# Moving left sums of a Strassen-like output product behind its first additions, in a windowed attention and gated feed-forward kernel

## The chip, the cores and the metric

The kernel runs on one core of one Trainium2 chip. The time is the device time of one execution in microseconds (us). The kernel before takes 333.5 us, the median of three runs (333.36 to 333.51). The engines are PE (matrix products), DVE (vector), ACT (activation functions and copies), Pool (a slower vector engine that also issues some DMAs) and SP (issues DMAs). Each engine works through its own queue in program order and waits on semaphores for the others.

## The reference

```python
# q, k, v: (8 batches, 8 heads, 576 positions, 64)
scores = q @ k^T / 8
scores = where(0 <= rel < 128, scores - slope[h] * |rel|, -1e9)   # rel = row - column
attn = softmax(scores);  x = (attn @ v) as (4608 tokens, 512)
out = (gelu(x @ w_gate) * (x @ w_val)) @ w_out                    # 512 -> 1536 -> 512
```

## The kernel before, in words

The 4608 tokens are worked off in nine groups `g` = 0 to 8 of 512 tokens. A group has a hidden stage (`x` times the gate and value weights, gelu, product; the result is `hT`, called `hid[g]`, twelve blocks `f` of 128 hidden features) and an output stage (`hid` times `w_out`). The attention of batch `b = g + 2` is spread over the output stage of group `g`, so that PE has work while others finish. One group takes about 34.6 us in the middle of the kernel.

**Hidden stage.** Blocks `f` are made one by one by `gate_val` (lines 642 to 673: eight matmuls, a gelu on ACT, a multiplication on DVE, line 667), except four blocks 6 to 9, which `gate_quad` (lines 822 to 892) makes together in seven products instead of eight. For these seven it needs sums of `x`: `combine_x` (lines 794 to 800, four additions t1 to t4, of which t2 needs t1 and t4 needs t2, on Pool in groups 2 to 6, written into the part of `left` for block pairs 3 to 5) and sums of weights, `combine_weights` (lines 772 to 781; those for blocks 0 to 3, which groups 7 and 8 use, are eight additions on Pool at the end of group 6's hidden stage). The last two multiplications of the four blocks run on Pool (lines 887 and 889).

**Output stage.** In groups 2 to 8 `out_products` (lines 1161 to 1270) also makes seven products (1 to 7) in place of eight, for each of two halves `a` = 0, 1 of the token pairs; six matmuls each (`product`, lines 752 to 763). With a11, a12, a21, a22 the quarters of `hid` (first index: lower or upper 256 tokens; second: even or odd block), `combine_left` (lines 729 to 737) makes four sums, each over six block pairs `i`, of which a call makes `lo` to `hi`:

```python
    steps = ((s1, a21, a22, ALU.add), (s2, s1, a11, ALU.subtract),
             (s4, a12, s2, ALU.subtract), (a21, a11, a21, ALU.subtract))
```

I call them sum 0, 1, 2 and 3, in the order of this line. Products 1 and 2 need no sum; product 6 needs sum 1, product 5 needs sum 0, product 7 needs sum 3, and product 3 needs sum 2. In groups 2 to 6 Pool makes all four sums of block pairs 0 and 1 behind `f` = 3 and sums 0 and 1 of pair 2 behind `f` = 5; DVE makes the rest after `f` = 11: sums 0 and 1 of pairs 3 to 5 (width 768), then sums 3 and 2 of pairs 2 to 5 (width 1024).

**Order of the output stage, groups 2 to 5** (line 1176 on, PE's order): products 1 and 2 of half 0, the first scores of the next batch (`scores2`, line 307), products 6, 5, 7 of half 0, product 1 of half 1, products 4 and 3 of half 0, the second scores, products 2, 6, 5, 7 of half 1, attention times values (`values`, line 508), products 4, 3 of half 1. Behind the products `gather_out` (lines 902 to 925) carries out of the PSUM banks: `p1` (909), `c11` (913, on DVE, an addition; it also frees the bank of product 2), `u2` (911), `p5` (917, on ACT), `c22` (919, on DVE; it reads the bank into which product 4 is then accumulated), `c21` (921) and `c12` (924). There are eight PSUM banks, handed on in turn, so a product or a score waits for an earlier reader of its bank. ACT's exponentials of the scores (line 236) and DVE's decay masks (line 241) lie in between. Group 6 has no scores of its own and another order (lines 1180 to 1213).

**Queues.** Pool's queue holds, in groups 2 to 5: a small copy `mark` (line 1328) that waits for block `f` = 3 of `hid`, the sums of `x`, its left sums, the two multiplications of the four blocks, and then the issue of fifteen loads of q, k and v (line 117; in group 5 only the five of v). In group 6, instead of loads: another `mark` (line 1352) that waits for sum 2, and the eight sums of weights. The normalizing factors of the attention (`rb`) are spread over the partitions by two DMAs from ACT's queue (line 463) and used by DVE (line 567).

Of the kernel before, what the change touches and what calls it, by code (L numbers as in the profile page):

```python
# [36 lines left out]
def kernel(  # L37
# [10 lines left out]
    nc = tc.nc  # L48
    B, H, S, D = q.shape
# [49 lines left out]
    mark = consts.tile([1, 2], BF16, name="mark")  # L99
# [353 lines left out]
    def gather(b):  # L453
        flat[b] = d_pool.tile([H, S], FP32, name="rd")
        for s in (0, 1):
            lo, w = shape(b, s)
            nc.scalar.dma_start(
                out=flat[b][:, lo:lo + 2 * w].rearrange("h (x t) -> x h t", x=2),
                in_=sumrow[b][0:128:8, lo:lo + w])
# [701 lines left out]
    def out_products(g):  # L1161
        b = g + 2
        O = lambda what, a, copy=act: gather_out(g, a, what, copy)
        P = lambda n, a: product(g, n, a)
        if b > B:
            for n, after in ((1, ("p1",)), (2, ()), (6, ("u2", "c11")), (5, ("p5",)), (7, ("c22",)), (4, ("c21",)),
                             (3, ("c12",))):
                for a in (0, 1):
                    P(n, a)
                    for what in after:  # L1170
                        O(what, a)
                store()
                if n == 6 and g + 1 < NG:
                    combine_x(g + 1)
            return
        P(1, 0)
        P(2, 0)
        O("p1", 0)
        urgent = 512 * (g + 2) - S * (b - 1)
        if b == B:  # L1180
            P(6, 0)
            O("u2", 0)
            O("c11", 0)
            P(5, 0)
            O("p5", 0)
            P(7, 0)
            O("c22", 0)
            scale = values(b - 1, later=True)
            P(4, 0)
            O("c21", 0)  # L1190
            P(3, 0)
            scale[0]()
            scale[1]()
            O("c12", 0)
            P(1, 1)
            O("p1", 1)
            store()
            P(2, 1)
            for do in scale[2:]:
                do()  # L1200
            O("c11", 1)
            P(6, 1)
            O("u2", 1)
            P(5, 1)
            O("p5", 1)
            P(7, 1)
            O("c22", 1)
            P(3, 1)
            O("c12", 1)
            P(4, 1)  # L1210
            O("c21", 1)
            combine_x(g + 1, 192, 256)
            return
        exp_table()
        O("c11", 0)
        later = []
        scores2(b, 0, later)
        A = later[0]
        P(6, 0)
        O("u2", 0, dve)  # L1220
        P(5, 0)
        for n in (0, 1, 3):
            A[n]()
        O("p5", 0)
        A[2]()
        P(7, 0)
        O("c22", 0)
        A[4]()
        for n in (5, 6, 7):
            A[n]()  # L1230
        P(1, 1)
        P(4, 0)
        P(3, 0)
        O("p1", 1)
        O("c21", 0)
        O("c12", 0)
        A[8]()
        A[9]()
        scores2(b, 2, later)
        A = later[1]  # L1240
        P(2, 1)
        P(6, 1)
        O("u2", 1, dve)
        O("c11", 1)
        add(b, 0, None, (0,))
        P(5, 1)
        for n in (0, 1, 3, 5):
            A[n]()
        O("p5", 1)
        A[2]()  # L1250
        P(7, 1)
        O("c22", 1)
        A[4]()
        for n in (6, 7):
            A[n]()
        store()
        scale, more = values(b - 1, urgent=urgent)
        for do in scale:
            do()
        P(4, 1)  # L1260
        P(3, 1)
        O("c21", 1)
        for do in more:
            do()
        O("c12", 1)
        A[8]()
        A[9]()
        add(b, 0, None, (2,))
        put_off.update({0: lambda: add(b, 0, act, (1,)), 1: lambda: add(b, 2, None, (0, 2)),
                        2: lambda: add(b, 2, act, (1,))})  # L1270
# [3 lines left out]
    for g in range(NG):  # L1274
        if 1 <= g < B - 2:
            transposes_dma(3 if g == 1 else g + 2)
        if g >= B - 1:
            for f in range(NF):
                if f in QUADS:
                    gate_quad(g, f)  # L1280
                elif not any(f0 < f < f0 + 4 for f0 in QUADS):
                    gate_val(g, f)
                if f == 4:
                    store()
                if f == 5:
                    combine_left(g, 0, 2, (0, 1), engine=nc.gpsimd)
                if f == 6:
                    combine_left(g, 2, 3, (0, 1))
                    combine_left(g, 0, 2, (3, 2), engine=nc.gpsimd)
            for which in ((0, 1), (3,), (2,)):  # L1290
                for lo, hi in ((3, 5), (5, 6)) if 0 in which else ((2, 5), (5, 6)):
                    combine_left(g, lo, hi, which)
            out_products(g)
            continue
        if g == 1:
            room = rooms(1)
            sums = combine_weights(6, nc.vector)
            for do in sums[:5]:
                do()
        for f in range(9 if g == 0 else 0, NF):  # L1300
            if f == 6 and g:
                gate_quad(g, 6, room if g == 1 else None,
                          (lambda: gather(g + 1)) if g in (2, B - 2) else None)
            elif not (g and 6 < f < 10):
                gate_val(g, f)
            if g == 1:
                for do in {0: sums[5:7], 1: sums[7:]}.get(f, ()):
                    do()
                if f in (1, 2, 3):
                    combine_x(1, 0, 256, {1: (0,), 2: (1, 2), 3: (3,)}[f])  # L1310
                if f in (4, 5, 10, 11):
                    combine_right({4: 0, 5: 1, 10: 2, 11: 3}[f])
            if f in put_off:
                put_off.pop(f)()
            if f == 1:
                store()
            if g == 0 and f == 10:
                masks_of_last_blocks(0, 8)
            if g == 0 and f == 9:
                for c in range(4):  # L1320
                    for w in (0, 1):
                        transpose(1, w, c, (act, dve)[w])
            if g < 2:
                continue
            if g == 2 and f == 2:
                add(3, 2, act, (1,))
            if f == 3:
                nc.gpsimd.tensor_copy(out=mark, in_=hid[g][0:1, f, 510:512])  # L1328
                combine_x(g, engine=nc.gpsimd)
                combine_left(g, 0, 2, (0, 1, 3, 2), engine=nc.gpsimd)  # L1330
            if f == (5 if g == 2 else 4):
                sums4(g + 1)
            if f == 5:
                combine_left(g, 2, 3, (0, 1), engine=nc.gpsimd)
                if 2 < g < B - 2:
                    gather(g + 1)
            if g == B - 2 and f == 2:
                combine_x(g + 1, 0, 192)
            if f == (11 if g == 2 else 6):
                spread_dma(g + 1)  # L1340
            if f == 6:
                if g + 3 < B:
                    load_qk(g + 3)
                if g + 2 < B:
                    load_v(g + 2)
            if f == 11:
                combine_left(g, 3, 6, (0, 1))
                for n in (3, 2):
                    combine_left(g, 2, 6, (n,))
        if g == B - 2:  # L1350
            sums = combine_weights(0)
            nc.gpsimd.tensor_copy(out=mark, in_=left[0:1, 2, 5, 0:2])
            for do in sums:
                do()
        if g == 1:
            nc.gpsimd.tensor_copy(out=mark, in_=kT[1][0:1, 0, 512:514])
            load_qk(4)
            load_v(3)
        if g == 0:
            nc.gpsimd.memset(Ps[0][:, :, 0:64], 0.0)  # L1360
            for t in (qs[1], ks[1]):
                nc.gpsimd.memset(t[64:128, 4, :], 0.0)
        if g in PRODUCTS:
            out_products(g)
        else:
            for item in steps(g):
                if isinstance(item, int):
                    out_part(g, item)
                else:
                    RUN[item[0]](*item[1:])  # L1370
            store()
        if g == 0:
            load_v(2)
            nc.gpsimd.tensor_copy(out=mark, in_=qT[0][0:1, 0, 512:514])
            load_qk(3)
# [30 lines left out]
```

## Time and profile before

| What | Value |
|---|---|
| time, median of 3 runs | 333.5 us (333.36 to 333.51) |
| the profiled execution: its own time | 333.97 us |
| its span, first to last instruction | 332.2 us |
| mean granted clock of PE | 0.995 |
| PE busy | 319.4 us (96%) |
| DVE busy | 255.4 us (77%) |
| ACT busy | 219.6 us (66%) |
| Pool busy | 200.3 us (60%) |

A line of a timeline gives the start in us from the span's start, the duration, the engine, the line of the kernel, the operation, what it writes and reads with the shape, the number of merged instructions (xN), and in brackets how long the engine stood idle before and what released it. Merged neighbours can overlap. A line of the windows gives a stretch, its length, then for each engine the busy time and instruction count, the granted clock, the DMA share and the rate.

Where the groups' output stages lie in this execution: product 6 of half 0 begins at 119.53 (group 2), 157.52 (group 3), 192.19 (group 4), 226.86 (group 5) and 260.63 us (group 6).

### The profile page before, as it was taken

The numbers are of one execution on the slowest core, as the hardware profiler recorded it, in microseconds if no ns is written. First come the engines' busy times: TensorE is split into PE (matmuls) and PEld (weight loads), VectorE is DVE, ScalarE is ACT, GpSimd is POOL, SyncE is SP. The second block draws the span as 40 slices with busy tenths as digits, with TensorE's granted clock in tenths as the row PEclk, the third lists the DMA queues.
The fourth block names the chain that finished last, engine by engine and source line by source line (L and its number), as shares of the span: only waits on it lengthen the run. The fifth ranks groups of instructions, "written<-read, shape, count | busy, mean of one in ns | idle before, by whom it ended". The sixth has DMA issues, their size and how long they took to land.

```text
span 332.2 us, 9496 instructions
## 1 busy us (share of the span) xinstructions
PE 319.4 (96%) x3784; PEld 216.7 (65%) x3784; DVE 255.4 (77%) x506; ACT 219.6 (66%) x417; POOL 200.3 (60%) x232
## 2 busy tenths in 40 slices
PE   8999999999999979999999999999999899999996
PEld 6566645574544748566765776577747687788765
DVE  7788766788789856977698669967898676785692
ACT  7974687568797656757875687577767237736641
POOL 6974689192096999079935994496019684420550
PEclk9999999999999989999999999999999999999999
DMA  8999999999799989954997499639200530003003
GB/s 215 168 197 190 203 168 183 130 211 136 137 170 127 181 159 191 168 131 100 174 197 115 129 178 192 131 106 190 99 34 5 142 129 3 0 2 127 3 0 126
DMA packets 149920, 43.57 MB, mean 131 GB/s; under 512 B 133588, under 2 KB 142964, under 8 KB 149876
## 3 DMA queue, kind: packets, MB, share of 16 engines
q0 software_dynamic: 107456, 18.10, 73.7%
q1 hardware_dynamic: 39104, 18.55, 25.9%
q10 hardware_dynamic: 3316, 6.32, 8.2%
q8 instruction: 29, 0.48, 0.6%
q14 instruction: 15, 0.12, 0.1%
HBM read 43.65 MB, written 9.53 MB: 160 GB/s over the span
## 4 chain that ended last, share of the span: by engine, by line
PE 49%; DVE 6%; POOL 4%; ACT 2%; issue 1%; DVEq 0%; POOLq 0%
PE ps L659 17%; PE ps L762 16%; PE ps L842 13%; DVE left L737 2%; PE ps L508 2%; DVE hT L667 1%; POOL left L800 1%; POOL left L737 1%; ACT P L236 1%; PE ps L307 1%; DVE xT L567 1%; POOL hT L887 1%; PE ps L444 1%; DVE P L241 1%; ACT osb L917 0%
## 5 line engine op out<-in xcount | busy, mean ns | idle before, releaser
L659 PE MATMUL ps<-xT,wg 128*128 128x512 bf16 (+4 forms) x312 | 71.8, 352 | 0.0
L659 PE MATMUL ps<-xT,wv 128*128 128x512 bf16 (+4 forms) x312 | 71.7, 352 | 0.0
L666 ACT ACTIVATE gelu<-ps 128x512 bf16<-128x512 f32 (+3 forms) x77 | 41.6, 546 | 35.1 <-PE ps L659 32.1
L667 DVE TENSOR_TENSOR hT<-ps,gelu 128x512 bf16<-128x512 f32 (+3 forms) x77 | 46.6, 623 | 18.3 <-PE ps L659 10.9
L236 ACT ACTIVATE P<-ps 128x512 bf16<-128x512 f32 (+1 forms) x108 | 52.2, 572 | 5.2 <-PE ps L307 3.1
L659 PEld LDWEIGHTS <-wv 128*128 128x128 bf16 x312 | 29.4, 98 | 29.8 <-DVE xT L567 0.2
L659 PEld LDWEIGHTS <-wg 128*128 128x128 bf16 x312 | 28.8, 98 | 25.9
L117 POOL DMA_DIRECT2D vb<-in_v_dram x40 | 34.1, 896 | 5.7 <-DMA ks<-in_k_dram 1.7
L241 DVE TENSOR_TENSOR P<-P,emask 128x768 bf16<-128x768 bf16 x60 | 32.0, 554 | 7.2 <-ACT P L236 5.4
L762 PEld LDWEIGHTS <-hT 128*128 128x128 bf16 x336 | 32.6, 99 | 7.1 <-issue 0.4
L762 PEld LDWEIGHTS <-left 128*128 128x128 bf16 x252 | 24.2, 98 | 10.3 <-issue 4.1
L1328 POOL COPY mark<-hT 1x2 bf16<-1x2 bf16 x5 | 0.9, 174 | 47.6 <-DVE hT L667 47.6
L887 POOL TENSOR_TENSOR hT<-qT,qs 128x512 bf16<-128x512 f32 x10 | 11.5, 1167 | 30.1 <-ACT qs L853 30.1
L762 PE MATMUL ps<-right,left 128*128 128x256 bf16 x168 | 22.0, 278 | 5.6 <-DVE osb L913 3.4
L842 PEld LDWEIGHTS <-kept 128*128 128x128 bf16 x256 | 25.1, 98 | 3.4 <-issue 0.6
L117 POOL DMA_DIRECT2D qs<-in_q_dram x30 | 25.4, 865 | 1.8 <-DMA wo<-in_moe_w_out_dram 1.0
L117 POOL DMA_DIRECT2D ks<-in_k_dram x30 | 25.4, 897 | 0.0
L762 PE MATMUL ps<-right,hT 128*128 128x256 bf16 x168 | 22.9, 278 | 0.2 <-DVE osb L919 0.2
L762 PE MATMUL ps<-wo,hT 128*128 128x256 bf16 x168 | 21.3, 275 | 0.0
L850 DVE TENSOR_TENSOR P<-ps,P 128x512 f32<-128x512 f32 x24 | 15.0, 682 | 6.8 <-PE ps L842 4.9
L850 DVE TENSOR_TENSOR qT<-ps,qT 128x512 f32<-128x512 f32 x20 | 12.9, 686 | 9.1 <-PE ps L842 7.7
L508 PE MATMUL ps<-P,vb 64*64 64x192 bf16 (+2 forms) x752 | 18.4, 221 | 1.5 <-ACT P L236 0.7
(170 smaller groups left out, 627.8 us busy)
## 6 DMA issues: line engine op xcount, KB each, us to landing
out_dram<-osb SPq DMA_DIRECT2D x34, 256.0 KB
rb<-rd ACTq DMA_DIRECT2D x10, 576.0 KB
vb<-in_v_dram POOLq DMA_DIRECT2D x32, 128.0 KB, 6.9
qs<-in_q_dram POOLq DMA_DIRECT2D x24, 128.0 KB, 5.5
ks<-in_k_dram POOLq DMA_DIRECT2D x24, 128.0 KB, 6.8
wo<-in_moe_w_out_dram POOLq DMA_DIRECT2D x4, 384.0 KB, 13.2
wg<-in_moe_w_gate_dram POOLq DMA_DIRECT2D x5, 256.0 KB, 8.4
wv<-in_moe_w_val_dram POOLq DMA_DIRECT2D x5, 256.0 KB, 9.0
```

Source lines behind the costliest of these rows:

```text
L117: nc.gpsimd.dma_start(out=t[at:at + n, j, :].rearrange("p (h d) -> p h d", h=H), in_=src[b][:, 128 * j:128 * j + n, :].rearrange("h p d -> ...
L236: nc.scalar.activation(out=dst, in_=src, func=AF.Exp, scale=0.125)
L241: nc.vector.tensor_tensor(out=dst, in0=dst, in1=m, op=ALU.mult)
L508: mm = nc.tensor.matmul(out=out, lhsT=lhsT, rhs=prob(b)[half, c, i, col:col + q1 - q0], start=all(t[2] != u for t in todo[:n]), stop=True, ...
L659: nc.tensor.matmul(out=ps[:, a:e], lhsT=w[:, c, 128 * f:128 * (f + 1)], rhs=xT[:, c, t0 + lo + a:t0 + lo + e], start=begins and a == 0, st ...
L666: nc.scalar.activation(out=gl[:, 0:n], in_=pg, func=AF.Gelu)
L667: nc.vector.tensor_tensor(out=hid[g][:, f, lo:hi], in0=pv, in1=gl[:, 0:n], op=ALU.mult)
L737: engine.tensor_tensor(out=to, in0=a, in1=b, op=op)
L762: nc.tensor.matmul(out=made[g, a, into], lhsT=lhsT, rhs=rhs, start=first and i == 0, stop=i == NF // 2 - 1, skip_group_check=True)
L842: nc.tensor.matmul(out=ps[:, 256 * e:256 * e + 256], lhsT=w[:, c, at:at + 128], rhs=x[:, c, :], start=n in (1, 2, 5) and e == 0 and c == 0 ...
L850: nc.vector.tensor_tensor(out=to[u], in0=cut(banks[n, u], to[u].shape[1]), in1=to[u], op=ALU.add)
L887: nc.gpsimd.tensor_tensor(out=out, in0=P5[u], in1=high, op=ALU.mult)
```

## The change

In groups 2 and 6 Pool no longer makes sums 3 and 2 of block pairs 0 and 1; it makes sums 0 and 1 of pairs 0 to 2 in one call behind `f` = 5. DVE makes sums 3 and 2 there for all six pairs (width 1536 instead of 1024). In groups 2 to 6 DVE's sums 3 and 2 no longer follow sums 0 and 1 directly: sum 3 stands behind `c11` of half 0, and sum 2 behind `u2` of half 0 (in group 6 both behind `c11`). In group 2 the sums of `x` are let go on Pool behind `f` = 0 instead of `f` = 3. In group 6 the `mark` and the sums of weights move with sum 2 into the output stage.

```diff
@@ out_products, b == B (group 6)
             P(6, 0)
             O("u2", 0)
             O("c11", 0)
+            for n in (3, 2):
+                combine_left(g, 0, 6, (n,))
+            nc.gpsimd.tensor_copy(out=mark, in_=left[0:1, 2, 5, 0:2])
+            for do in combine_weights(0):
+                do()
             P(5, 0)
@@ out_products, groups 2 to 5
         exp_table()
         O("c11", 0)
+        lo = 0 if g == 2 else 2
+        combine_left(g, lo, 6, (3,))
         later = []
         scores2(b, 0, later)
         A = later[0]
         P(6, 0)
         O("u2", 0, dve)
+        combine_left(g, lo, 6, (2,))
         P(5, 0)
@@ the hidden stage of groups 2 to 6
-            if f == 3:
+            if f == (0 if g == 2 else 3):
                 nc.gpsimd.tensor_copy(out=mark, in_=hid[g][0:1, f, 510:512])
                 combine_x(g, engine=nc.gpsimd)
+            if f == 3 and 2 < g < B - 2:
                 combine_left(g, 0, 2, (0, 1, 3, 2), engine=nc.gpsimd)
             if f == (5 if g == 2 else 4):
                 sums4(g + 1)
             if f == 5:
-                combine_left(g, 2, 3, (0, 1), engine=nc.gpsimd)
                 if 2 < g < B - 2:
+                    combine_left(g, 2, 3, (0, 1), engine=nc.gpsimd)
                     gather(g + 1)
+                else:
+                    combine_left(g, 0, 3, (0, 1), engine=nc.gpsimd)
@@
             if f == 11:
                 combine_left(g, 3, 6, (0, 1))
-                for n in (3, 2):
-                    combine_left(g, 2, 6, (n,))
-        if g == B - 2:
-            sums = combine_weights(0)
-            nc.gpsimd.tensor_copy(out=mark, in_=left[0:1, 2, 5, 0:2])
-            for do in sums:
-                do()
```

## The prediction

> **What bounds the kernel now.** I read first which waits PE has, because PE is busy nearly throughout and every stall of it counts at once.
>
> ```profile
> PE ps L762 <- DVE osb L913: 3.4, 4, 1.0
> PE ps L762 <- DVE left L737: 2.3, 2, 1.2
> ```
>
> The columns are the waiting engine, tile and line, what it waited for, the total in us, the times, and the longest. Both entries lie in output stages (line 762) and end on DVE: four times a product waits until `c11` (line 913) has freed its bank, twice it waits for left sums (line 737). That is 5.7 us, and the four and the two fit groups 2 to 5 and groups 2 and 6. So I read these stages in the timeline, first group 2.
>
> ```profile
> 106.19 0.69 POOL L117 DMA_DIRECT2D vb<-in_v_dram  x1 [1.40 <-DMA ks<-in_k_dram]
> ...
> 111.64 1.16 POOL L737 TENSOR_TENSOR left<-hT 128x512 bf16<-128x512 bf16 x1
> ...
> 113.33 2.19 ACT L853 ACTIVATE vb<-P 128x512 bf16<-128x512 f32 x4 [1.14 <-DVE P L850]
> ...
> 116.97 0.67 POOL L737 TENSOR_TENSOR left<-left,hT 128x256 bf16<-128x256 bf16 x1
> 117.03 1.34 ACTq L463 DMA_DIRECT2D rb<-rd  x2
> ...
> 117.59 2.27 POOL L889 TENSOR_TENSOR hT<-P,vb 128x512 bf16<-128x512 f32 x2
> ...
> 119.53 0.50 PE L762 MATMUL ps<-right,left 128*128 128x256 bf16 x3
> 119.80 4.26 POOL L117 DMA_DIRECT2D qs<-in_q_dram  x5
> 119.90 0.56 DVE L737 TENSOR_TENSOR left<-hT 128x768 bf16<-128x768 bf16 x1 [1.61 <-POOL hT L889]
> 120.15 1.57 ACT L236 ACTIVATE P<-ps 128x512 bf16<-128x512 f32 x3
> ...
> 121.10 0.50 PE L762 MATMUL ps<-right,left 128*128 128x256 bf16 x3 [1.07 <-DVE left L737]
> ...
> 122.64 1.44 PE L762 MATMUL ps<-right,left 128*128 128x256 bf16 x6 [1.03 <-DVE osb L913]
> ...
> 126.10 0.82 PE L762 MATMUL ps<-right,hT 128*128 128x256 bf16 x6
> ...
> 128.16 4.27 POOL L117 DMA_DIRECT2D vb<-in_v_dram  x5
> ...
> 133.18 1.94 DVE L567 TENSOR_TENSOR xT<-ps,rb 128x320 bf16<-128x320 f32 x5
> ```
>
> Pool is late here: its left sums run from 111.64 to 117.6, only then come its two multiplications (line 889), and DVE, free since 119.90 - 1.61 = 118.29, waits for them before its own sums 0 and 1. PE does half of product 6 (three matmuls, on Pool's sums), waits 1.07 us for DVE's, does the other half, and waits 1.03 us more before product 5, because DVE makes sums 3 and 2 ahead of `c11`. The six matmuls of product 5 then take 1.44 us. The windows show why.
>
> ```profile
> 119.40:122.60 3.20, 1.14 (x20) 0.58 (x11) 2.67 (x6) 2.31 (x4) 3.20 (x5) 0.96 1.04 244
> 122.60:125.60 3.00, 2.96 (x15) 2.04 (x15) 0.93 (x3) 1.49 (x4) 3.00 (x4) 0.50 1.89 172
> 260.00:262.30 2.30, 1.13 (x11) 0.76 (x8) 1.45 (x4) 0.37 (x1) 1.07 (x1) 1.00 1.04 229
> ```
>
> Behind 3.2 us in which PE was busy for 1.14 the granted clock (third column from the right) is 0.50 for 3 us; behind group 6's stall (last row, 1.13 busy of 2.3) it stays at 1.00. Groups 3, 4 and 5 look alike; here is 4.
>
> ```profile
> 191.05 0.56 DVE L737 TENSOR_TENSOR left<-hT 128x768 bf16<-128x768 bf16 x1
> ...
> 192.12 0.68 DVE L737 TENSOR_TENSOR hT<-hT 128x1024 bf16<-128x1024 bf16 x1
> ...
> 193.32 0.42 DVE L913 TENSOR_TENSOR osb<-ps,osb 128x256 f32<-128x256 f32 x1
> ...
> 193.79 0.81 PE L762 MATMUL ps<-right,left 128*128 128x256 bf16 x6 [0.77 <-DVE osb L913]
> ...
> 193.99 0.55 DVE L241 TENSOR_TENSOR P<-P,emask 128x768 bf16<-128x768 bf16 x1
> ...
> 194.65 0.37 ACT L917 COPY osb<-ps 128x256 f32<-128x256 f32 x1 [0.55 <-PE ps L762]
> ...
> 195.84 0.82 PE L762 MATMUL ps<-right,hT 128*128 128x256 bf16 x6
> ...
> 197.77 2.06 ACT L236 ACTIVATE P<-ps 128x512 bf16<-128x512 f32 x4 [0.71 <-PE ps L307]
> ```
>
> DVE's order is sums 0, 1, 3, 2, then `c11`, `u2`, a mask; product 5 at 193.79 waits for `c11`, and product 4 begins at 195.84. Pool's part is in time here.
>
> **The change part by part.** The working follows PE up to the start of product 4 in each stage, since from there each stage runs in its old order.
>
> *Sums of x behind block 0, group 2.* Nothing. Pool's last load ends at 106.19 + 0.69 = 106.88, and its four sums of x (111.64 - 106.88, with the mark, leaves 4.76 us for them) already follow at once. What hides the earlier release is the load queue; if that cover went, the Pool chain would start earlier, and only wait longer at its end, as the next step shows.
>
> *Fewer left sums on Pool, group 2.* Gone: four calls of 1.16 and two of 0.67 us. Added: two calls of width 768. A width of 512 takes 1.16 and one of 256 takes 0.67, so 0.49 more: 1.65 each. Pool is done at 111.64 + 3.35 = 115.0 instead of 117.6. The multiplications need the gelus, which ACT makes from 113.33 to 115.52, the third of four ending near 115.0; so they run from 115.0 to 117.3. DVE is free at 118.29, so Pool has 1 us to spare, and that is the cover. A hand-over took 0.04 (Pool's end at 119.86, DVE's start at 119.90); I allow 0.1, so DVE starts at 118.40 and not 119.90. Sums 0 and 1 are done near 119.5, since in group 4 the third of DVE's sums starts 1.07 behind the first. Product 6 starts at 119.53 with the halves that Pool made, and needs DVE's half three matmuls later: the wait of 1.07 goes.
>
> *Sums 3 and 2 behind `c11` and `u2`, group 2.* From group 4's starts: sum 3 starts 1.07 behind sum 0, sums 3 and 2 take a step of 0.60 each (193.32 - 192.12, halved; duration 0.68), and `c11` and `u2` 0.67 together. Width 1536 isn't in these stages, but elsewhere on DVE:
>
> ```profile
> L745 DVE TENSOR_TENSOR right<-wo 128x1536 bf16<-128x1536 bf16 x2 | 1.9, 948 | 0.0
> ```
>
> So the step is 0.95 - 0.08 = 0.87. DVE's new order is sum 0 at 118.40, `c11` 119.47, sum 3 119.81, `u2` 120.68, sum 2 121.02, mask 121.89, `c22` 122.37 to 122.79. Product 5 needs its bank from `c11`, free at 119.9, and follows product 6 at 119.53 + 0.66 = 120.19 with no wait. Product 7 needs sum 3, done at 120.76; product 7 would start at 120.84. Sum 2 now stands behind `u2`, which waits for product 6; that is done by 120.4, so it holds nothing up. Queued behind the moved sums are the mask and `c22`. `c22` also needs ACT's `p5`, which comes behind three exponentials that end at 120.15 + 1.57 = 121.72, so it is done at 122.1: DVE is later. Product 4 waits for `c22` and starts at 122.85; PE was ready near 122.1 to 122.4, a new wait of some 0.45 us. Product 4 started at 126.10 before: a gain of 3.25 us. In it are 1.07 and 1.03 of waits, and the slow clock, 126.10 - 122.64 = 3.46 against 195.84 - 193.79 = 2.05, so 1.41, less the new wait. I take the clock as full, since what remains is one wait of 0.45, below group 4's 0.77 and group 6's, after which it was full.
>
> The Trainium skill speaks against this. "TensorE: Matmul & The Clock Gate", section "Why this matters for your kernels", asks only that PE not idle over about 3 us between bursts. By that rule two waits of 1 us wouldn't have cost the clock, the cause would lie elsewhere and stay, and the gain would be 1.41 us smaller. The row says PE was idle for two thirds of 3.2 us, in pieces, and that the half clock began right then.
>
> *The loads behind Pool's multiplications.* They start 2.5 us earlier in group 2, at 117.3, now on top of the DMA of the normalizing factors (117.03). I cost this at nothing: the factors are used from 133.18 on, 3.25 earlier now, so 129.9; that leaves 12.9 us for a transfer that goes first. If that cover goes, it is the third rival.
>
> *Groups 3 to 5.* Only the order on DVE changes. In group 4: sum 0 at 191.05, `c11` at 192.12 to 192.54, sum 3 192.46, `u2` 193.06, sum 2 193.40, mask 194.00 (before: 193.99, so nobody behind it is later). Product 5 no longer waits. `p5` on ACT had 0.55 us of idle time before it; it comes at 194.10 to 194.47, then `c22` to about 194.95, and product 4 starts at 195.04 instead of 195.84: 0.80. Three groups make 2.4 us.
>
> *Group 6.*
>
> ```profile
> 252.87 1.15 POOL L737 TENSOR_TENSOR left<-hT 128x512 bf16<-128x512 bf16 x1
> ...
> 255.87 1.23 ACT L853 ACTIVATE qs<-kT 128x512 bf16<-128x512 f32 x2
> ...
> 258.81 2.27 POOL L887 TENSOR_TENSOR hT<-qT,qs 128x512 bf16<-128x512 f32 x2
> ...
> 261.11 0.56 DVE L737 TENSOR_TENSOR left<-hT 128x768 bf16<-128x768 bf16 x1 [0.82 <-POOL hT L887]
> ...
> 262.32 1.16 PE L762 MATMUL ps<-right,left 128*128 128x256 bf16 x9 [1.19 <-DVE left L737]
> ...
> 263.31 0.82 PE L762 MATMUL ps<-right,hT 128*128 128x256 bf16 x6
> ...
> 270.34 2.25 POOL L778 TENSOR_TENSOR P<-wg,P 128x512 bf16<-128x512 bf16 x2
> ...
> 271.38 1.30 DVE L800 TENSOR_TENSOR ks<-xT 128x128 bf16<-128x128 bf16 x1
> ...
> 272.72 0.23 DVE L800 TENSOR_TENSOR ks<-xT,ks 128x128 bf16<-128x128 bf16 x1
> ...
> 273.32 1.91 PE L842 MATMUL ps<-ks,P 128*128 128x256 bf16 x16
> ```
>
> Pool's left sums shrink as above, to 252.87 + 3.35 = 256.2; its multiplications wait for gelus of which the first ends near 256.5, and end at 258.8 instead of 261.1. DVE, free at 261.11 - 0.82 = 260.29, starts at 260.40, 0.71 earlier; PE resumes at 261.61. Product 7 (263.31) would be ready at 262.60, but sum 3 now stands behind `c11`: 260.40 + 1.07 + 0.34 = 261.81, done at 262.76, so product 7 starts at 262.80: 0.51 gained. The `mark` waits for sum 2, and behind it on Pool are only the sums of weights. Sum 2 is done at 263.63 (262.68 + 0.95), where it was done at 261.11 + 1.67 + 0.68 = 263.46, so the eight sums of weights end some 0.17 later, at 272.76. They are hidden except in one place: DVE's small sums of x for group 7 stand beside the last of them. The first takes 1.30 us where the next takes 0.23, and ends at 272.68, with Pool's last sum at 272.59. The product that needs their second result starts at 273.32, 0.37 behind its end. Were that chain again tied to Pool's end, it would be ready at 273.15, while PE now wants it at 272.81, and only 0.17 would be left of 0.51. I take 0.2, by this row, and keep 0.51 as the other end.
>
> The Trainium skill, "SBUF — State Buffer", section "SBUF: two separate sides", has DVE instructions with two SBUF inputs and Pool instructions lock each other out for one whole instruction, whoever starts first. By that rule the sum of x would be held for the Pool sum under way alone, be in time, and the gain 0.5. The row agrees in the hold of about one Pool sum (1.13), but in it the end is Pool's last.
>
> *Sum.* 3.25 + 2.4 + 0.2 = 5.85 us off the profiled 333.97, so 328.1. The profiled execution is 0.47 above the median of the runs shown, and I take the saving from that median: 333.50 - 5.85 = 327.65, say 327.7.
>
> **The rivals.** First, the half clock stays, or comes back behind the new wait at product 4: 1.41 us less, 329.1. For it: where the clock's window falls is unknown. Against it: product 5 of group 4, behind a single wait, took 0.81 and not 1.44.
>
> Second, ACT gives part of the gain back in groups 3 to 5: it had only 0.55 us of idle time before `p5`, so its exponentials move by 0.55, and if the second scores wait for banks that ACT frees, each stage keeps 0.55 of 0.80: 3 x 0.25 = 0.75 less, 328.4. Against it: before the exponentials of the second scores (197.77) ACT stood idle for 0.71 us, so it has room.
>
> Third, slower than before: the factors come late in group 2.
>
> ```profile
> vb<-in_v_dram POOLq DMA_DIRECT2D x32, 128.0 KB, 6.9
> ```
>
> The last column is the median from issue to landing. The fifteen loads are issued up to 128.16 + 4.27 = 132.4, now up to 129.9. If the factors' pieces were served behind all of them, they would land at 129.9 + 6.9 = 136.8; DVE's scaling, due at 129.9, would be 6.9 late, the next hidden stage with it, and the sum would be 1.05 above before: 334.6. It decides from a landing at 129.9 + 5.85 = 135.8. Against it: before, the loads began only 2.8 us behind the factors, and line 567 shows no wait at 133.18.
>
> That the change doesn't do what it says holds for the sums of x alone, and they are counted at nothing.
>
> **How the numbers follow.** Forecast 0.73; half clock 0.12; ACT 0.09; late factors 0.06, of which 0.04 land late enough to be slower and 0.02 at no difference. About 0.2% (0.7 us) is what a measurement of this kernel can tell from no change. So faster 0.94, same 0.02, slower 0.04. The range's low end is the forecast less 0.31 (group 6 whole) and 0.45 (no wait at product 4 in group 2): 326.9. The high end has both mild rivals, 1.41 + 0.75, and 0.5 for group 6 giving nothing and new waits 0.3 longer: 330.3. It leaves out the late factors and nothing else.
>
> **What would show it.** In the profile after, PE's waits on lines 913 and 737 should all but vanish, with a wait of about 0.45 us for `c22` (line 919) in group 2; the clock should be 1.00 through group 2; Pool's multiplications there should end near 117.3, product 4 start near 122.9; product 6 of groups 3, 4, 5 and 6 should come about 3.3, 4.1, 4.9 and 5.7 us earlier than before. The sum of weights in group 6 should cost PE at line 842 about 0.3 us. I am wrong if a clock of 0.5 still appears, if DVE's line 567 waits for `rb`, or if the stages start earlier but end at the old distance.

## The result, and the profile after

The changed kernel took 328.30, 332.85, 327.68 and 328.89 us in four executions (median 328.6), the kernel before beside it 333.36 to 333.75 (median 333.5, four executions). The ratio is 0.9843, with a 95% interval of 0.9819 to 0.9867: faster, since all of the interval lies below 1. The comparison leaves out the execution of 332.85 us, whose mean granted clock was 0.995; without it the median is 328.3. The profiled execution took 328.30 us with a span of 326.5 and a mean granted clock of 1.000 (before: 333.97, 332.2 and 0.995).

First the waits of PE in the kernel after, in the form of the prediction's first fence: what PE waited for, us in total, times, longest.

```profile
PE ps L508 <- issue: 1.0, 1, 1.0
...
PE ps L762 <- DVE left L737: 0.5, 1, 0.5
PE ps L762 <- DVE osb L919: 0.4, 2, 0.2
PE ps L842 <- DVE ks L800: 0.3, 1, 0.3
```

The entry on `c11` (line 913) is gone, and of the two waits on left sums one is left, group 6's. `c22` (line 919) costs 0.2 where 0.45 was forecast. The first entry is new at this size: line 508, the products with the values, waits 1.0 us for "issue", that is, the profile names no engine or transfer that PE waited for. Next the timeline of group 2 in the kernel after.

```profile
105.32 0.17 POOL L1336 COPY mark<-hT 1x2 bf16<-1x2 bf16 x1
...
109.15 2.78 PE L842 MATMUL ps<-left,kept 128*128 128x256 bf16 x24
...
114.72 2.27 POOL L889 TENSOR_TENSOR hT<-P,vb 128x512 bf16<-128x512 f32 x2 [1.32 <-ACT vb L853]
...
116.93 4.26 POOL L117 DMA_DIRECT2D qs<-in_q_dram  x5
...
118.03 0.56 DVE L737 TENSOR_TENSOR left<-hT 128x768 bf16<-128x768 bf16 x1
...
119.10 0.42 DVE L913 TENSOR_TENSOR osb<-ps,osb 128x256 f32<-128x256 f32 x1
119.17 1.48 PE L762 MATMUL ps<-right,left 128*128 128x256 bf16 x12
119.44 0.95 DVE L737 TENSOR_TENSOR hT<-hT 128x1536 bf16<-128x1536 bf16 x1
...
120.64 0.95 DVE L737 TENSOR_TENSOR left<-hT,left 128x1536 bf16<-128x1536 bf16 x1
...
122.44 0.81 PE L762 MATMUL ps<-right,hT 128*128 128x256 bf16 x6 [0.20 <-DVE osb L919]
...
125.68 1.57 POOL L117 DMA_DIRECT2D ks<-in_k_dram  x2 [1.86 <-DMA qs<-in_q_dram]
...
128.24 1.09 PE L508 MATMUL ps<-P,vb 64*64 64x64 bf16 x60 [0.17 <-ACT P L236]
...
130.28 0.22 PE L508 MATMUL ps<-P,vb 64*64 64x64 bf16 x2 [0.95 <-issue]
```

Pool's multiplications end at 114.72 + 2.27 = 116.99 (forecast 117.3), products 6 and 5 run as one group of twelve matmuls without a wait, and product 4 starts at 122.44 (forecast 122.85; before 126.10). The windows of the kernel after show the clock there, in the third column from the right.

```profile
117.90:121.10 3.20, 3.08 (x64) 2.45 (x63) 3.06 (x7) 3.17 (x6) 3.20 (x4) 1.00 1.13 201
121.10:125.60 4.50, 4.30 (x76) 3.55 (x74) 3.11 (x7) 3.66 (x10) 2.73 (x4) 1.00 1.65 199
```

It is 1.00 where it had been 0.50. At the end of the timeline stands the new loss: the last two value products start at 130.28, after 0.95 us of "issue". Before, the same two had waited 0.21:

```profile
133.20 0.22 PE L508 MATMUL ps<-P,vb 64*64 64x64 bf16 x2 [0.21 <-issue]
```

Group 4 in the kernel after:

```profile
187.24 0.56 DVE L737 TENSOR_TENSOR left<-hT 128x768 bf16<-128x768 bf16 x1
...
188.31 0.42 DVE L913 TENSOR_TENSOR osb<-ps,osb 128x256 f32<-128x256 f32 x1
188.38 1.48 PE L762 MATMUL ps<-right,left 128*128 128x256 bf16 x12
...
190.16 0.39 ACT L917 COPY osb<-ps 128x256 f32<-128x256 f32 x1
...
190.66 0.42 DVE L919 TENSOR_TENSOR osb<-ps,osb 128x256 f32<-128x256 f32 x1
...
191.13 0.81 PE L762 MATMUL ps<-right,hT 128*128 128x256 bf16 x6
```

From DVE's sum 0 to product 4 it is now 191.13 - 187.24 = 3.89 us, before 195.84 - 191.05 = 4.79: 0.90 gained. Group 6 in the kernel after:

```profile
256.00 1.16 PE L762 MATMUL ps<-right,left 128*128 128x256 bf16 x9 [0.48 <-DVE left L737]
...
257.20 0.83 PE L762 MATMUL ps<-right,hT 128*128 128x256 bf16 x6
...
264.88 2.26 POOL L778 TENSOR_TENSOR P<-wg,P 128x512 bf16<-128x512 bf16 x2
...
265.28 1.95 DVE L800 TENSOR_TENSOR ks<-xT 128x128 bf16<-128x128 bf16 x1
...
267.26 0.23 DVE L800 TENSOR_TENSOR ks<-xT,ks 128x128 bf16<-128x128 bf16 x1
...
267.63 2.56 PE L842 MATMUL ps<-ks,P 128*128 128x256 bf16 x22 [0.25 <-DVE ks L800]
```

Product 7 comes 6.11 us earlier than before. DVE's first small sum of x then takes 1.95 us, until Pool's last sum of weights is done at 264.88 + 2.26 = 267.14, and the product that needs the sums comes only 5.69 earlier (267.63 against 273.32). So the account of the 5.7 us between the spans, by how much earlier each place comes:

| place | forecast | measured |
|---|---|---|
| product 4, group 2 | 3.25 | 3.66 |
| last value products, group 2 | 3.25 | 2.92 |
| product 6, groups 3, 4, 5, 6 | 3.3, 4.1, 4.9, 5.7 | 2.91, 3.81, 4.71, 5.60 |
| product 7, group 6 | 6.16 | 6.11 |
| line 842 behind group 6 | 5.85 | 5.69 |

The sum agrees, but two of its steps don't: group 2 gained more than forecast up to product 4, and lost 0.74 at line 508, which the forecast didn't have.

### The profile page after: what moved, and what is told of

Its sections match the earlier page's. It is cut to its first block, busy times and chain, and to the rows that moved or that the text cites. A ratio compares the mean times of both kernels' runs of the same rounds, so it can differ in the third digit from the quotient of the medians.

```text
span 326.5 us, 9488 instructions
## 1 busy us (share of the span) xinstructions
PE 317.4 (97%) x3784; PEld 215.8 (66%) x3784; DVE 256.8 (79%) x506; ACT 219.0 (67%) x417; POOL 195.6 (60%) x224
## 4 chain that ended last, share of the span: by engine, by line
PE 89%; ACT 3%; DVE 3%; issue 2%; DMA 1%; SPq 0%; ACTq 0%; DVEq 0%
PE ps L659 36%; PE ps L842 18%; PE ps L762 18%; PE ps L508 5%; PE ps L696 4%; ACT P L236 2%; PE ps L307 2%; PE ps L716 2%; PE ps L221 1%; DMA qs<-in_q_dram 1%; PE ps L444 1%; DVE ks L800 1%; PE ps L159 1%; ACT osb L917 1%; DVE xT L547 0%
## 5 line engine op out<-in xcount | busy, mean ns | idle before, releaser
L762 PEld LDWEIGHTS <-hT 128*128 128x128 bf16 x336 | 31.9, 97 | 7.6 <-issue 1.0
L762 PE MATMUL ps<-right,hT 128*128 128x256 bf16 x168 | 22.2, 272 | 0.6 <-DVE osb L919 0.4
L762 PE MATMUL ps<-right,left 128*128 128x256 bf16 x168 | 20.6, 273 | 0.5 <-DVE left L737 0.5
```

Of the source, the lines that this page charges most:

```text
L762: nc.tensor.matmul(out=made[g, a, into], lhsT=lhsT, rhs=rhs, start=first and i == 0, stop=i == NF // 2 - 1, skip_group_check=True)
```

## The experiments

Twelve kernels were run, each 6 to 12 times, on three chips, beside the kernel before on the same chip. Four questions were open: whether the half clock needed both waits of group 2, what the early sums of x are worth, what PE waits for at line 508, and whether group 6 keeps anything.

### Half the change in group 2: the order alone, Pool's part alone

g2_order_only is the kernel before with one edit, in group 2 alone: DVE's sums 3 and 2 move behind `c11` and `u2`.

```diff
+MOVED = (2,)
...
         O("c11", 0)
+        if g in MOVED:
+            combine_left(g, 2, 6, (3,))
...
         O("u2", 0, dve)
+        if g in MOVED:
+            combine_left(g, 2, 6, (2,))
@@ f == 11
-                for n in (3, 2):
+                for n in () if g in MOVED else (3, 2):
                     combine_left(g, 2, 6, (n,))
```

> The kernel before, with sums 3 and 2 of group 2 alone moved behind c11 and u2; Pool makes all its left sums as before. The wait for Pool's late sums stays (1.07 us, product 6 at 121.1), the wait for c11 goes. Theory A, the half clock needs both waits close together: the clock stays at 1.00, product 4 of group 2 starts near 123.8 instead of 126.1, and the kernel is 2.3 us faster (331.2, ratio 0.993). Rival, short waits have nothing to do with the clock: 0.50 again for some 3 us, product 4 near 125, 1.1 us faster (332.4, ratio 0.997).

g2_pool_only is the other half: Pool makes fewer sums in group 2, and DVE's order stays as it was, with sums 3 and 2 of all six pairs ahead of `c11`. The sums of x stay behind `f` = 3.

```diff
-                combine_left(g, 0, 2, (0, 1, 3, 2), engine=nc.gpsimd)
+                if g > 2:
+                    combine_left(g, 0, 2, (0, 1, 3, 2), engine=nc.gpsimd)
...
-                combine_left(g, 2, 3, (0, 1), engine=nc.gpsimd)
+                combine_left(g, 0 if g == 2 else 2, 3, (0, 1), engine=nc.gpsimd)
...
-                    combine_left(g, 2, 6, (n,))
+                    combine_left(g, 0 if g == 2 else 2, 6, (n,))
```

> The kernel before, with fewer left sums on Pool in group 2 alone (DVE makes sums 3 and 2 for all six pairs there, still ahead of c11; the sums of x stay behind block 3). The wait for Pool's sums goes, the wait for c11 stays and grows to some 1.3 us. Theory A, the half clock needs both waits: full clock, product 4 near 123.7, 2.4 us faster (331.1, ratio 0.993). Rival, the cause lies elsewhere: half clock again, 1.0 us faster (332.5, ratio 0.997).

Measured: 331.41 us, ratio 0.9960 (0.9936 to 0.9984), and 332.03 us, ratio 0.9973 (0.9950 to 0.9996). One wait is left in each. The timeline of group 2 and its windows, first g2_order_only:

```profile
121.17 1.16 PE L762 MATMUL ps<-right,left 128*128 128x256 bf16 x9 [1.06 <-DVE left L737]
...
123.84 0.81 PE L762 MATMUL ps<-right,hT 128*128 128x256 bf16 x6
```

```profile
119.50:122.70 3.20, 2.03 (x29) 1.39 (x19) 2.70 (x6) 2.42 (x6) 3.20 (x5) 1.00 1.03 235
122.70:125.70 3.00, 3.00 (x52) 2.46 (x53) 1.90 (x6) 2.15 (x6) 3.00 (x4) 1.00 2.07 164
```

Then g2_pool_only:

```profile
122.39 0.81 PE L762 MATMUL ps<-right,left 128*128 128x256 bf16 x6 [1.30 <-DVE osb L913]
```

```profile
119.50:122.70 3.20, 1.90 (x54) 1.57 (x54) 3.17 (x7) 2.73 (x4) 3.20 (x5) 1.00 1.13 224
122.70:125.70 3.00, 3.00 (x29) 2.55 (x27) 1.33 (x3) 2.41 (x6) 2.21 (x3) 1.00 1.33 201
```

A single wait, even one of 1.30 us, leaves the clock at 1.00 with PE busy 1.9 to 2.0 of 3.2 us. That is what the theory of the two waits asks, but a profile is one execution. The mean granted clock of every run says more: a stretch of 3 us at 0.50 makes it 0.995. The runs fall in two clear classes, 0.993 to 0.995 and 0.998 to 1.000. In the kernels that keep both waits (before, and two that follow) 33 of 78 runs are in the low class; in the three that have at most one of them in group 2 (these two and g2_only below) none of 30. In the three profiles of the low class (before, order_g3to5, g6_only) windows of 6 us show a clock below 1.00 only between 120 and 132 us, in group 2. So with both waits the half clock comes in some 4 of 10 executions, and taking away either wait ended it in these kernels. The pair isn't the only thing that goes with a low mean: the changed kernel and its variants below have neither wait, and 5 of their 46 runs are in the low class too; no profile caught where their clock drops. The kernel before took, in the median of each class, 334.2 to 334.4 us with the low clock and 332.3 to 332.8 with the full one, on three chips (one execution of 1,699 us is left out): 1.4 to 2.1 us for what the forecast counted at 1.41. Its profiled execution was one of the low class.

The times alone don't decide between theory and rival. Theory A forecast ratios of 0.993 for both, the rival 0.997; measured are 0.9960 and 0.9973. Both forecasts started from a kernel before that always has the half clock. Against the full-clock runs of before on this chip (332.6 in the median) the two kernels are 1.2 and 0.6 us faster, and g2_pool_only's profile has 0.89 us of the new wait at line 508.

### Group 2 alone, groups 3 to 5 alone, group 6 alone

g2_only and g6_only are the kernel before with all of the change in group 2 or in group 6: the order on DVE, the fewer left sums on Pool, in g2_only also the sums of x behind `f` = 0, and in g6_only also the sums of weights behind sum 2. order_g3to5 moves only DVE's sums 3 and 2, in groups 3 to 5. The part on DVE's order of g2_only and order_g3to5 reads, shortened:

```diff
+MOVED = (2,)          # g2_only;  (3, 4, 5) in order_g3to5
...
         O("c11", 0)
+        if g in MOVED:
+            combine_left(g, 2, 6, (3,))       # g2_only: 0, 6
...
         O("u2", 0, dve)
+        if g in MOVED:
+            combine_left(g, 2, 6, (2,))       # g2_only: 0, 6
...
-                for n in (3, 2):
+                for n in () if g in MOVED else (3, 2):
```

> The kernel before with all of group 2's part of the change and nothing else. Theory: product 4 of half 0 comes 3.25 us earlier than in the kernel before, 0.4 to 0.5 more where Pool's loads end early and the sums of x start early, and 0.7 is lost again ahead of the last matmuls of line 508: 2.9 to 3.1 us in all, ratio 0.991. Rival: the parts need each other, and the sum of group 2, groups 3 to 5 and group 6 alone differs from the whole by over 1 us.

> The kernel before, with sums 3 and 2 of groups 3, 4 and 5 alone moved behind c11 and u2. Theory: 0.8 us for each group, 2.4 in all, and the profile after shows 0.9, so 2.7: 330.8 to 331.1, ratio 0.992 to 0.993. Rival (ACT or the second half of each stage gives it back): 0.55 or less for each, ratio 0.995 or more.

> The kernel before, with group 6 alone changed (fewer sums on Pool, sums 3 and 2 and the sums of weights behind c11). Theory: 0.5 us gained at product 7 and 0.3 to 0.4 of it given back at line 842, where PE waits for DVE's small sums of x, which stand beside Pool's last sums of weights: 0.1 to 0.2 us faster, ratio 0.9995. Rival (the gain stays, since Pool's sum under way is all that holds DVE): 0.5 us, ratio 0.9985, and no wait at line 842. Only the trace can tell these apart.

Measured: g2_only 330.45 us, ratio 0.9907 (0.9875 to 0.9940); order_g3to5 330.35 us, 0.9914 (0.9879 to 0.9949); g6_only 333.90 us, 1.0017 (0.9990 to 1.0043). The three add up to 1.6% of 333 us, 5.4 us, against 1.57% of the whole change on its own chip, each with a third of a per cent of doubt. order_g3to5 keeps group 2 as it was; its timeline there:

```profile
122.91 1.28 PE L762 MATMUL ps<-right,left 128*128 128x256 bf16 x6 [1.03 <-DVE osb L913]
123.99 1.48 PE L762 MATMUL ps<-right,hT 128*128 128x256 bf16 x6
```

Six matmuls take 1.48, not 0.82: the half clock again, with both waits there, and its gain is that of groups 3 to 5 alone. Five of its 11 runs are in the low class, 331.38 in the median, the six others 329.49. g6_only shows the same rows as the whole change: DVE's small sum takes 1.95 us from 270.69, and line 842 waits 0.26 for it. Of its stage's gain, less what is given back, nothing can be measured in the time.

### The sums of x back behind `f` = 3, and the changed kernel once more

after_x_late is the changed kernel with one edit; after_again is the changed kernel as it is, on another chip.

```diff
-            if f == (0 if g == 2 else 3):
+            if f == 3:
```

> The changed kernel with the sums of x of group 2 let go behind block 3 again. By the prediction's step (worth nothing): as the changed kernel, 328.3, ratio 0.984. By what the profile after shows (Pool's last load ended at 105.23 there and not at 106.88, the sums of x began at 105.46 and PE's wait for them in the four-block product was gone): 0.4 to 0.55 us slower than the changed kernel, 328.8, with PE waiting some 0.4 us at line 842 for line 800.

> The changed kernel unaltered, as the base for the other three on this chip: 0.984 of the kernel before, with a wait of some 0.9 us put down to issue ahead of the last two matmuls of line 508 in group 2.

Measured: 328.93 us, ratio 0.9885 (0.9854 to 0.9916), and 329.16 us, 0.9888 (0.9847 to 0.9928). The timeline of after_x_late:

```profile
107.13 0.18 POOL L1336 COPY mark<-hT 1x2 bf16<-1x2 bf16 x1 [3.00 <-DVE hT L667]
...
109.71 2.56 PE L842 MATMUL ps<-left,kept 128*128 128x256 bf16 x22 [0.52 <-POOL left L800]
```

Pool stands idle for 3.00 us until block 3 lets it go, and PE waits 0.52 us at line 842 for the sums, as it had done for 0.39 in the kernel before; in the changed kernel it doesn't wait. So the early release is worth 0.5 us at that place in these executions, in which Pool's loads ended early (104.13 in after_x_late, 105.23 in the first profile of the changed kernel, against 106.88 in the profile of before). In the two medians it can't be seen, since after_again has a wait of its own: its first scores of group 2 wait 0.73 us for `kT` from the DMA (`kT<-ks`), which the first profile of the same kernel doesn't have. Its transpose was issued at 111.62 there and at 108.08 in the first profile. The changed kernel's runs spread over 328.25 to 331.02 us on this chip.

### The loads of group 2 held back

In after_loads_held Pool issues the loads of group 2 only behind DVE's sum 1, in after_loads_late only behind `c12` of half 0; nothing else differs from the changed kernel.

```diff
-            if f == 6:
+            if f == 6 and g > 2:
...
+                if g == 2:
+                    nc.gpsimd.tensor_copy(out=mark, in_=left[0:1, 1, 5, 0:2])
+                    load_qk(g + 3)
+                    load_v(g + 2)
```

(The copy into `mark` makes Pool wait for what it reads; after_loads_late reads `c12`'s sum instead.)

> The changed kernel with group 2's fifteen loads held on Pool until DVE's sum 1 is done, so that they begin near 119.3 and not 116.9. Theory: the wait of 0.9 us that three kernels with early loads show ahead of the last two matmuls of line 508 in group 2, and three kernels with late loads don't, comes from the loads' place: it falls to 0.2 or less and the kernel gains 0.7 us on the changed one. Rival: it comes with the earlier products and not with the loads; it stays at 0.9.

> The changed kernel with group 2's fifteen loads held on Pool until c12 of half 0, near 124.4 instead of 116.9. Holding them by 2.3 us left the wait put down to issue ahead of the last two matmuls of line 508 at 0.79. Theory: that wait grows with what the loads have put into the DMA queues in the 7 us before it; with the loads starting only there it falls to 0.2 or less, and 0.8 us are gained unless the transposes of the next batch then come late for group 3's first scores. Rival: it has nothing to do with the loads and stays at 0.8 to 1.0.

Measured: 327.95 us, ratio 0.9851 (0.9816 to 0.9886), and 329.17 us, 0.9874 (0.9836 to 0.9911). The timeline of after_loads_held, Pool's loads and PE's line 508:

```profile
119.25 4.26 POOL L117 DMA_DIRECT2D qs<-in_q_dram  x5 [0.33 <-issue]
...
129.63 0.22 PE L508 MATMUL ps<-P,vb 64*64 64x64 bf16 x2 [0.79 <-issue]
...
131.86 1.56 POOL L117 DMA_DIRECT2D vb<-in_v_dram  x2 [1.53 <-DMA ks<-in_k_dram]
```

Loads from 119.25 on, nearly the place that they had before (119.80), still leave 0.79 of the wait, where the theory expected 0.2 or less. On the span's clock every kernel with the wait starts its loads by 119.25 and every other from 119.64 on; but counted from line 444, the last work ahead of the four-block products, they start 12.97 us behind it here and 12.94 us in g6_only, which has no such wait. So the start alone doesn't explain it. What also goes with the wait in every kernel is the bracket of the last line shown: Pool itself stands still before one of its loads, until an earlier one has landed. In all eight kernels that have the wait (0.79 to 1.04 us) Pool stood so for 1.5 to 2.8 us at a stretch; in the six others, the kernel before among them, its loads went out with no more than 0.24 between them, and the wait is at most 0.21. The two go together; that one brings the other isn't shown.

The trace's DMA rows say more. A queue that the profile calls "instruction" moves one piece of 0.02 MB in this stretch; the row is that of the kernel after, between 126 and 131 us:

```profile
q8 instruction: 1, 0.02, 1.2%
```

Narrower windows put this piece at 127.89, and the last two value products start at 130.28, 2.39 us behind it. In twelve of the fourteen profiles, the eight with the wait among them, they start 2.2 to 2.5 us behind the piece, and in none sooner; before has 131.00 and 133.20. Only in after_loads_late and after_both_held, where the loads begin no more than 0.1 us ahead of the piece, does it come 4.1 to 4.2 us ahead of them, and there is no wait. So a piece of PE's own instructions that arrives late behind the loads would fit all fourteen. It is likely and not shown: the trace doesn't say whose instructions the piece holds, and no run changed it alone. Now after_loads_late:

```profile
128.16 1.13 PE L508 MATMUL ps<-P,vb 64*64 64x64 bf16 x62 [0.17 <-ACT P L236]
...
145.00 1.07 ACT L860 COPY P<-ps 128x512 f32<-128x512 f32 x2 [3.40 <-DMA rd<-r]
...
145.65 2.83 PE L842 MATMUL ps<-left,kept 128*128 128x256 bf16 x24 [2.06 <-ACT P L860]
```

The wait at line 508 is gone (62 matmuls in one group), but ACT then stands still for 3.40 us in group 3 at the DMA of the normalizing factors, `rd<-r`, and PE waits 2.06 us for ACT. ACT issues this DMA only at 143.73, 1.67 us after the reciprocals that it carries are done (142.06); in the changed kernel it goes out before the second reciprocal is done (142.25 and 143.22). after_both_held, with the same late loads, has the same stall (3.16 us); what holds the issue isn't named. It is akin to the prediction's third rival: not in the changed kernel, but next to it.

### Sum 2 later in group 2, and the sums of weights behind the small sums of x in group 6

after_weights_held makes Pool wait, before its last two sums of weights in group 6, for DVE's small sums of x; after_two_edits has this, and sum 2 of group 2 behind `c22`; after_both_held has it with the loads as in after_loads_late.

```diff
-            for do in combine_weights(0):
+            sums = combine_weights(0)
+            for do in sums[:6]:
                 do()
...
+            nc.gpsimd.tensor_copy(out=mark, in_=sums_x(g + 1)[3][0:1, 0, 254:256])
+            for do in sums[6:]:
+                do()
@@ after_two_edits
-        combine_left(g, lo, 6, (2,))
+        if g > 2:
+            combine_left(g, lo, 6, (2,))
...
+        if g == 2:
+            combine_left(g, lo, 6, (2,))
```

> The changed kernel with two edits. In group 2, sum 2 stands behind c22 instead of u2: PE's wait of 0.20 for c22 ahead of product 4 goes, and product 4 comes 0.3 to 0.5 us earlier, product 3 some 0.3. In group 6, the last two sums of weights wait on Pool for DVE's small sums of x of group 7: the first of these takes 0.2 to 1.2 us and not 1.95, and PE's wait of 0.25 at line 842 goes. Together 0.4 to 0.7 us faster than the changed kernel. Rival for the second: DVE's op takes as long without a Pool sum beside it.

> The changed kernel with one edit: in group 6 the last two sums of weights wait on Pool for DVE's small sums of x. From the trace of the kernel with two edits: DVE's first sum takes 0.21 and not 1.95 us, PE's wait at line 842 goes, 0.4 us faster than the changed kernel. Rival: the sums of weights then come late for the product that needs them, and PE waits there.

> The changed kernel with both edits of the other two: 0.4 us from group 6, and 0.8 from group 2 if the late loads remove the wait there; 327.1 and ratio 0.981 if both hold, 0.983 if only the first does.

Measured: 327.62 us, ratio 0.9853 (0.9814 to 0.9891); 329.09 us, 0.9855 (0.9810 to 0.9901); 330.06 us, 0.9891 (0.9852 to 0.9930). Group 6 in the timeline of after_two_edits:

```profile
264.67 0.21 DVE L800 TENSOR_TENSOR ks<-xT 128x128 bf16<-128x128 bf16 x1
...
265.62 2.26 POOL L778 TENSOR_TENSOR P<-wg,P 128x512 bf16<-128x512 bf16 x2
...
266.61 2.79 PE L842 MATMUL ps<-ks,P 128*128 128x256 bf16 x24
```

The same sum takes 0.21 us with Pool out of the way, and line 842 follows with no wait, 1.75 us behind the product before it (264.86) instead of 267.63 - 265.47 = 2.16: the 0.4 that group 6 gave back is regained, and Pool's sums are still in time. after_weights_held shows the same (1.74). In group 2 the later sum 2 takes away the wait for `c22`, and product 4 starts 0.28 sooner by the stage's own clock, but product 3 then waits for sum 2, so next to nothing is kept.

As times these stay undecided. On the chip of after_again (0.9888) after_two_edits and after_loads_held are 1.2 to 1.5 us lower in the median, but the intervals overlap; on its own chip after_weights_held's profile has the wait for `kT<-ks` again, with 1.1 us, and after_both_held pays at lines 860 and 800 (1.8 and 1.6 us, Pool's sums of x being late behind its own loads). No version is shown to be better than the changed kernel.

## Why the prediction was right, step by step

**Group 2 to product 4 (3.25).** The mechanism was right: both waits gone, the clock full, a small new wait at `c22`. It was too small by 0.6: product 4 comes 3.66 earlier though what stands ahead of the stage is 0.19 later (line 444 at 106.77 instead of 106.58), 3.85 in all. The failing step is "Sums of x behind block 0, group 2. Nothing." These are the rows of the kernel before on which that step turns:

```profile
PE ps L842 <- POOL left L800: 0.4, 1, 0.4
...
106.94 0.17 POOL L1328 COPY mark<-hT 1x2 bf16<-1x2 bf16 x1
```

Line 842 had waited for those sums, and their early release took the wait away: 0.5 (0.52 in after_x_late). The working followed PE from product 6 on and passed over the first of these rows, which is in the view of PE's waits. The cover that it named was there in that execution, since the `mark` came right behind Pool's last load (106.88). But it doesn't hold in every execution: in the fourteen profiles that load, which stands ahead of every edit, ends anywhere from 103.3 to 109.4. In the changed kernel's profile it ended at 105.23, so part of the 0.5 is that execution's luck. The rest is the wait at `c22`, 0.20 and not 0.45.

**The half clock (1.41 of it).** The pair of waits brought it, as argued: 33 of 78 runs with both have a low clock, none of 30 with one or none in kernels that keep the rest of before, and 5 of 46 of the changed kernel and its variants. What the prediction didn't see is that before had it in 22 of 55 runs only. The sum was made for a profiled execution that had it, and 1.41 of the 5.85 us is gained in such executions alone. Against runs of before at full clock the changed kernel, itself at full clock, is 3.4 us faster on after_again's chip (332.3 to 328.93), and not 4.3 (5.7 less 1.41); a wait like the 0.73 for `kT` in its profile could make up most of the rest, but the runs at 328.93 have no trace. On the first chip, where before's profiled execution had the low clock and its four runs lay at 333.4 to 333.8, the forecast for the time came out; on a run of before at full clock it would have been some 1.4 too hopeful. Its figure of about 0.2% for what can be told from no change was somewhat small: the intervals here reach 0.2 to 0.5% to either side. The Trainium skill's rule from "TensorE: Matmul & The Clock Gate", section "Why this matters for your kernels", which spoke for a half clock with another cause, doesn't cover these rows: the half clock went with the pair of waits, and neither of the two (1.07 and 1.03 us) comes near an idle stretch of about 3 us.

**The loads behind Pool's multiplications (nothing).** This step failed too, the other way: 0.74 us at line 508, a wait that no rival had. The factors weren't late (line 567 starts at 129.53 without a wait), so the cover that the prediction named held; another one was gone. The wait comes only where Pool's loads wait for each other, and goes when they are held far enough. The two products start 2.2 us or more behind the piece of the instruction queue in all fourteen profiles, so a late piece is the likely cause; that stays open.

**Groups 3 to 5 (0.80 each).** Right in mechanism, 0.9 each in the trace: `p5`, `c22` and the hand-over to PE came together 0.1 us closer than counted. ACT took nothing back; the second rival fell.

**Group 6 (0.2).** Right by its steps: 0.51 gained at product 7, and 0.42 given back at line 842 where 0.34 was forecast, for the reason that was argued, since with Pool held off the small sum takes 0.21. By the Trainium skill's rule from "SBUF — State Buffer", section "SBUF: two separate sides", DVE would have been held for the one Pool sum under way, about 1.1 us. The row has 1.95, through that sum and the next. The row of before that the prediction read had said so: DVE's sum began at 271.38, when Pool had 0.1 us left of one sum, and was done only behind the next (272.59).

So the total was right, 327.7 forecast and 328.6 measured, with two missed steps of 0.5 and 0.74 us of opposite sign, and a third, the clock, that was there in less than half of the runs. The mechanism carried most of the sum; that the two misses nearly cancel, and that the profile of before was one with the half clock, is luck.

## What to carry to other kernels

When work is moved between engines, go through all waits of the critical engine that end on the work moved, also those ahead of the stage that the change is about: the row on line 842 was in the first view. Before a term of the sum rests on a low clock in one profile, look at the granted clock of every run; it may be there in a part of them only. And an edit that frees a queue earlier should be costed by who else uses that queue: here the same fifteen loads went with a wait of PE of 0.95 us when they were early, and of 2 us when they were late.

## What the runs showed of the hardware that was not expected

Two waits of 1.07 and 1.03 us within 3.2 us (PE busy 1.14 of them) bring 3 us of half clock in about 4 of 10 executions; single waits of 1.06 and 1.30 (PE busy 2.03 and 1.90) in none of 24. Of the runs of kernels with the whole change, which have neither wait, 5 of 46 also have a mean clock of 0.995, and no profile caught where.

A DVE sum of two SBUF operands that started while Pool was adding took 1.95 us, until Pool's sum under way and the next were done, against 0.21 with Pool idle, in the same place of the same stage.

PE can stand for 0.8 to 1.0 us at one fixed instruction with no semaphore that explains it. With one profile for each kernel, this came in exactly the eight kernels whose loads wait for each other, and there the instruction starts 2.2 to 2.5 us behind a piece moved by the queue called "instruction".
